# Splitting the first stage of a fused attention and gated-product kernel into two passes through DRAM

## The chip, the cores and the metric

The kernel runs on one core of a Trainium2 chip. The metric is the device time of one execution in microseconds (us). Three runs of the kernel before took 1695.24, 1697.13 and 1695.3 us; the median is 1695.3 us.

## What is computed

The reference, cut to what matters (8 batches, 8 heads, 576 positions, 64 columns a head; 4608 tokens of 512 columns; widths 1024 and 1536):

```python
k_p, v_p = mean of k, v over groups of 8 positions        # 72 keys
attn = softmax(q @ k_p.T / 8)                             # 576 x 72 per head
x = attn @ v_p, heads side by side                        # 4608 x 512
h = (x @ w1) * (x @ w2)                                   # 4608 x 1024
y = h @ w3 @ w_out                                        # 4608 x 512
xn = y / sqrt(mean(y*y) + 1e-6) * rms_g
out = (silu(xn @ w_gate) * (xn @ w_val)) @ w_out2         # 4608 x 512
```

The weights and the MoE inputs arrive as 64-bit floats, so every weight is converted on the chip.

## The kernel before, in words

**Products.** Every large product is made of three matmuls (`mm3`, lines 86 to 89): both operands are split into a high part (rounded to the matmul's type) and a low part (the rest), and high by high, high by low and low by high are summed in PSUM. A split (`split`, lines 82 to 84) is one copy on ACT and one subtraction on DVE. The 4608 tokens are worked on in 9 blocks of 512 (index i, `NB`), the 1024 columns of h in 8 strips of 128 (index m, `KF1`).

**Prelude.** w3 @ w_out is folded into one matrix first (lines 540 to 583): w3 is loaded, converted (`Conv`, lines 97 to 154), transposed on PE and multiplied by w_out. The result, split, stays in SBUF as `wph` and `wpl` (four tiles of pool `wC`) for the whole first stage. A list of side steps, `aux`, is laid between these matmuls: the attention of batch 0, the conversion of the first half of w1 and w2, and the gate products of strips 0 to 3 of block 0 (`ab0`), kept in SBUF as `hf0`.

**First stage.** `ab(i, m, s)` (lines 633 to 642) is 12 matmuls: strip m of x @ w1 (s = 0, then ACT copies it out) or of x @ w2 (s = 1, then DVE multiplies it by the copy); the product h is split into `hh`, `hl`. `y_mm(i, m)` (through `second`, lines 462 to 471) is another 12 matmuls: strip m of h times the folded matrix, into four PSUM banks that gather over the 8 strips. `Pipe.run` (lines 654 to 675) walks m: gate products of strip m, then `y_mm` of strip m-1, and after each piece a tick of a `Ticker`. The ticks spread the attention of the next batch over the block: `att_of(i)` (lines 644 to 652) is a list of some 35 short steps for 20 ticks. A block thus has 288 product matmuls, 192 of gate products and 96 of the second product. When the 8 strips are done, `y_end` (lines 586 to 626) copies y to `ydram`, and squares and sums it for the norm.

**Attention.** For each of 5 tiles of 128 positions (the last 64): `step_Q` transposes q on PE; `step_S` (two halves) multiplies by the pooled keys on PE, takes the maximum on DVE, and makes 4 exponentials a half on ACT; `step_N` divides on DVE; `step_T` transposes the result, on PE for batches 0 and 1, and for the others with 12 block transposes on DVE a full tile (lines 340 to 347). `av_step` multiplies by the pooled values and writes the split x of the next block. `pool_four` and `pool_sum` load and pool k and v.

**Second stage, weights.** w_gate and w_val are converted, combined into 8 forms (`gv_jobs`, lines 744 to 794, function `sums`: four subtractions, and for each of two column halves a split of 128x1024 and two writes to `wdram` on the POOL queue), 12 groups in all. This and the conversion of w_o2 (`o2_jobs`) are the list `prep`, ticked through during blocks 7 and 8 of the first stage and the start of the second (lines 1129 to 1138). `ring_load` brings the forms back from `wdram`, `o2_load` w_o2.

**Second stage, products.** Block 0 is computed plainly (`gv`, `o_mm`; lines 1139 to 1171), then pairs of blocks through `quad` and `o_part` to the end.

**Order.** Each engine works in one order; SP and POOL issue DMAs in order, so an issue that waits for a buffer or for data holds up those behind it. The framework's scheduler turns the program's order into the engines' orders by its own plan, so a step can move a little.

Of the kernel before, what the change touches and what calls it, by code (L numbers as in the profile page):

```python
# [1 line left out]

# [18 lines left out]
def kernel(  # L21
# [17 lines left out]


    nc = tc.nc
# [30 lines left out]

    def ftile(dt=F32):
        return f_p.tile([P, 512], dt, tag="f", name="f")
# [15 lines left out]

# [91 lines left out]
    rdram = dram_p.tile([NB, TB], F32, name="rdram")  # L182
    ones_f = const.tile([P, 1], F32, name="ones_f")
# [3 lines left out]


# [48 lines left out]
    def att_steps(b):  # L237
# [14 lines left out]
        def step_k1():  # L252
            load_q(0)
# [3 lines left out]
            load_q(1)  # L257

        def step_kT():
            ps = psum()  # L260
            kp = st8.pop(("kp", b))
            for p in range(NP):
                nc.tensor.transpose(
                    ps[:, p * SP : (p + 1) * SP], kp[:, p * P : (p + 1) * P], ident[:SP, :SP]
                )
            pv = ps[:, : NP * SP].rearrange("d (p s) -> d p s", p=NP)
            nc.scalar.activation(kT[:D, :, :SP], pv[:D], AF.Copy, scale=ATT_SCALE)
            nc.scalar.activation(kT[D:, :, SP:], pv[D:], AF.Copy, scale=ATT_SCALE)

        def step_Q(g, hf):  # L270
# [8 lines left out]
            if hf < nu:  # L279
                ps = psum()  # L280
# [13 lines left out]
        def step_S(t, hf):  # L294
            s0, n = TILES[t]
            ps = psum()
# [38 lines left out]
        def step_T(t, hf):  # L335
# [12 lines left out]
            ps = psum()  # L348
# [15 lines left out]

        pre = [step_k0, step_k1]
        steps = [step_kT, lambda: step_Q(0, 0), lambda: step_Q(0, 1)]
        for t in range(NTL):

            def a(t=t):
                step_S(t, 0)  # L370

            def bq(t=t):
                step_Q(t // 2 + 1, t % 2)

            def c(t=t):
                step_S(t, 1)

            def d(t=t):
                if t > 0:
                    step_T(t - 1, 0)  # L380
                step_N(t)

            def e(t=t):
                if t > 0:
                    step_T(t - 1, 1)

            steps += [a, bq, c, d, e]
        steps[4:4] = [load_v]
        steps[11:11] = [step_v]
        steps += [lambda: step_T(NTL - 1, 0), lambda: step_T(NTL - 1, 1)]  # L390
        return pre, steps

    def av_step(b, i, p):
# [4 lines left out]
        ps = psum()  # L398
# [63 lines left out]
    def second(i, m, wh, wl, last, tok_major):  # L462
        hh, hl = h_t.pop((i, m))
        if m == 0:
            yacc[i] = [py_p.tile([P, 512], F32, tag="y", name="y") for _ in range(4)]
# [37 lines left out]
    hf0 = [preA_p.tile([P, 512], F32, name=f"hf0_{m}") for m in range(4)]  # L503
# [26 lines left out]
    def ab0(m, s):  # L530
        xh, xl = xtile(0)
        if s == 0:
            nc.scalar.copy(hf0[m], mm_feat(w1h, w1l, xh, xl, m))
        else:
            pb = mm_feat(w2h, w2l, xh, xl, m)
            nc.vector.tensor_tensor(out=hf0[m], in0=pb, in1=hf0[m], op=ALU.mult)
# [11 lines left out]
    aux = atts[0][0] + atts[0][1][:-2] + c0[:2] + atts[0][1][-2:]  # L548
# [3 lines left out]
    aux += [lambda m=m, s=s: ab0(m, s) for s in range(2) for m in range(4)]  # L552
    aux += atts[1][0]
# [5 lines left out]
    for n in range(NW3):  # L559
# [73 lines left out]
    def ab(i, m, s):  # L633
        wh, wl = ((w1h, w1l), (w2h, w2l))[s]
        ps = mm_feat(wh, wl, *xtile(i), m)
        if s == 0:
            a0[i, m] = ftile()
            nc.scalar.copy(a0[i, m], ps)
        else:
            hf = ftile()  # L640
            nc.vector.tensor_tensor(out=hf, in0=ps, in1=a0.pop((i, m)), op=ALU.mult)  # L641
            split_h(i, m, hf)

    def att_of(i):
        steps = av_steps(i, i + 1)
        if i + 1 < B:
            steps = steps + atts[i + 1][1][:-2]
            if i + 2 < B:
                steps = steps + atts[i + 2][0]
            steps = steps + atts[i + 1][1][-2:]  # L650
            steps = steps + av_steps(i + 1, i + 1)
        return steps

    class Pipe:


        def __init__(self):
            self.pend, self.todo = None, []

        def fin(self):  # L660
            if self.pend is not None:
                self.todo += self.pend()
                self.pend = None

        def run(self, i, ms, wide, second, tick):
            for m in ms:
                for s in range(2):
                    wide(i, m, s)
                    if self.todo:
                        self.todo.pop(0)()  # L670
                    tick()
                self.fin()
                tick()
                self.pend = lambda m=m: second(i, m)
            tick.flush()

    pipe = Pipe()
    c1 = conv_steps([load_w12(n) for n in range(8, 16)], 2)
    for m in range(4):
        split_h(0, m, hf0[m])  # L680
        y_mm(0, m)
    preB.close()
    preA.close()
    x1_p = ctx.enter_context(tc.tile_pool(name="x1", bufs=1))
    wA_p = ctx.enter_context(tc.tile_pool(name="wA", bufs=4))
    pools[1] = x1_p
    col_tiles(wA_p, W12, (w1h, w1l, w2h, w2l))
    cv = Ticker(c1, 1)
    cv.run(6)
    tick = Ticker(att_of(0), 14)  # L690
    for m in range(4, KF1):
        ab(0, m, 0)
        cv.step()
        tick()
    cv.flush()
    for m in range(4, KF1):
        ab(0, m, 1)
        tick()
        pipe.fin()
        tick()  # L700
        pipe.pend = lambda m=m: y_mm(0, m)
    tick.flush()
    xt.pop(0)

    for i in range(1, NB - 2):
        pipe.run(i, range(KF1), ab, y_mm, Ticker(att_of(i), 3 * KF1 - 4))
        xt.pop(i)

    for st in att_of(NB - 2):
        st()  # L710
    att.close()
    r_p = ctx.enter_context(tc.tile_pool(name="r", bufs=5, side="right"))

# [25 lines left out]
    o2r = {}  # L739

    def rtile(nm, dt=F32R):
        return r_p.tile([P, 2048], dt, tag="r", name=nm)

    def gv_jobs(G, s, kp):
        cell = {}
        w = (w_gate, w_val)[s]

        def quart(z):
            if "f" not in cell:
                cell["f"] = rtile("wf", F32).rearrange("p (j f c) -> p j f c", j=2, f=8)  # L750
# [3 lines left out]
        def sums(_):  # L754
            f = cell.pop("f")

            def q(n):
                return f[:, :, FI[n], :]

            for o, x, y in (  # L760
# [5 lines left out]
                nc.vector.tensor_tensor(out=q(o), in0=q(x), in1=q(y), op=ALU.subtract)  # L766
            for j in range(2):
                c = 2 * G + j
                st = rtile("wst").rearrange("p (f l c) -> p f l c", f=8, l=2)
                nc.scalar.copy(st[:, :, 0, :], f[:, j])  # L770
                nc.vector.tensor_tensor(
                    out=st[:, :, 1, :],
                    in0=f[:, j],
                    in1=st[:, :, 0, :].bitcast(F32),
                    op=ALU.subtract,
                )
                for z in range(2):
                    nc.gpsimd.dma_start(
                        out=wdram[s, c, z][:, :, kp],
                        in_=st[:, 4 * z : 4 * z + 4].bitcast(F32),  # L780
                    )
                ready.add((s, c, kp))

        def view(z):
            return z.rearrange("p (j f c) -> p j f c", j=2, f=2)

        def src(z):
            k0 = (2 * z + kp) * P
            return w[k0 : k0 + P, G * 512 : (G + 1) * 512]

        return [
            Conv(src(0), raw_p, out=lambda: quart(0), view=view),
            Conv(src(1), raw_p, out=lambda: quart(1), view=view, then=sums),
        ]

    def o2_jobs(g):
# [7 lines left out]
        def done(_):  # L804
            f = cell.pop("f")
            hi, lo = o2r[g] = [wtile(wC_p, nm) for nm in ("oh", "ol")]
            split(hi, lo, f)
            nc.gpsimd.dma_start(out=odram[g][0], in_=hi.bitcast(F32))
            nc.gpsimd.dma_start(out=odram[g][1], in_=lo.bitcast(F32))

        return [
            Conv(
                w_o2[(4 * g + j) * P : (4 * g + j + 1) * P, :],
                raw_p,
# [5 lines left out]

    prep = []
    for G in range(3):
        for s in range(2):
            for kp in range(2):
                prep += gv_jobs(G, s, kp)
    for g in range(3):
        prep += o2_jobs(g)
    for j, cv_ in enumerate(prep):
        cv_.on_act = True
        if j % 5 > 2:  # L830
            cv_.pool = (r_p, "xq", 2)
    prep = conv_steps(prep, 4)

# [22 lines left out]
    o2_n = [3]  # L856
# [13 lines left out]
    def xn_load(i, c):  # L870
        if c == 0:
            xr[i] = ftile()
            nc.sync.dma_start(out=xr[i], in_=rdram[i].partition_broadcast(P))
        r = raw_p.tile([P, 1024], I32, tag="raw", name="raw").bitcast(F32)
        xr[i, c] = r.rearrange("p (k t) -> p k t", k=2)
        nc.sync.dma_start(
# [353 lines left out]
```

## Time and profile before

| what | us or share |
|---|---|
| median of 3 runs | 1695.3 |
| profiled execution: span from first to last instruction | 1693.5 |
| profiled execution's own time: the span with some 1.8 us around it, by the runs | about 1695.3 |
| PE busy | 1619.1 (96%) |
| DVE busy | 1037.3 (61%) |
| ACT busy | 663.9 (39%) |
| POOL busy | 90.8 (5%) |
| DMA, mean over the span | 159 GB/s |

How to read it: PE's busy time is a union of matmuls that overlap each other, so it tells where PE had nothing at all to do, not how densely it ran; a lone matmul of 128x512 shows some 0.39 us, yet in a dense stretch they start every 0.23 us. The count of matmuls in a stretch and its length say more. DVE and ACT shares are close to what they say, as their instructions hardly overlap.

### The profile page before, as it was taken

What the parts mean: (1) busy time and instruction counts of PE and PEld (TensorE: products, weight loads), DVE (VectorE), ACT (ScalarE), POOL (GpSimd) and SP (SyncE); (2) the same over time, 40 slices, a digit from 0 to 9 for tenths busy, and PEclk for the clock granted to TensorE, in tenths of its full rate; (3) what the DMA queues carried; (4) which work ended last, traced back from release to release, by engine and by line L of the source; (5) the groups of instructions that cost most, each with busy time, mean ns of one, the idle gap of its engine ahead of it and who ended that gap; (6) DMA issues with size and microseconds to landing.
All of it is one profiled execution on the core that took longest, in us unless ns stands there. A gap on an engine that the chain in (4) does not pass through costs nothing.

```text
span 1693.5 us, 19782 instructions
## 1 busy us (share of the span) xinstructions
PE 1619.1 (96%) x7252; PEld 1275.7 (75%) x7252; DVE 1037.3 (61%) x1850; ACT 663.9 (39%) x1604; POOL 90.8 (5%) x104
## 2 busy tenths in 40 slices
PE   6898999999999999998798999999999999999999
PEld 3466677777777778776676888888888888888887
DVE  7875475757585858677756653476355735465344
ACT  3654543334333334455543243243333334233321
POOL 0001010100000000031310000000000000000000
PEclk9999999999999999999999999999999999999999
DMA  9854340413131310297968774367455746455422
GB/s 261 217 144 100 47 102 28 82 34 77 39 71 44 65 48 6 84 323 257 334 223 328 286 270 159 141 247 253 164 194 186 257 165 224 149 201 212 182 101 75
DMA packets 125588, 270.07 MB, mean 159 GB/s; under 512 B 50858, under 2 KB 77482, under 8 KB 109364
## 3 DMA queue, kind: packets, MB, share of 16 engines
q1 hardware_dynamic: 104916, 227.89, 39.8%
q0 software_dynamic: 20576, 40.92, 9.4%
q8 instruction: 57, 0.93, 0.2%
q14 instruction: 39, 0.32, 0.1%
HBM read 218.39 MB, written 50.37 MB: 159 GB/s over the span
## 4 chain that ended last, share of the span: by engine, by line
PE 47%; DMA 3%; DVE 0%; ACT 0%; issue 0%; SPq 0%; ACTq 0%
PE ps L87 9%; PE ps L88 9%; PE ps L89 9%; PE o L89 5%; PE o L88 5%; PE o L87 5%; DMA wr<-wd 2%; PE y L88 2%; PE y L89 2%; PE y L87 2%; DMA raw<-in_moe_w_out_dram 0%; DMA ydram<-f 0%; DVE f L596 0%; DVE hl L84 0%; ACT f L591 0%
## 5 line engine op out<-in xcount | busy, mean ns | idle before, releaser
L87 PE MATMUL ps<-xf,wr 128*128 128x512 f32 x576 | 224.1, 389 | 0.0
L89 PE MATMUL ps<-xf,wr 128*128 128x512 f32 x576 | 224.1, 389 | 0.0
L88 PE MATMUL ps<-xf,wr 128*128 128x512 f32 x576 | 224.1, 389 | 0.0
L89 PE MATMUL o<-oh,hcl 128*128 128x512 f32 x384 | 149.6, 389 | 0.0
L87 PE MATMUL o<-oh,hch 128*128 128x512 f32 x384 | 149.4, 389 | 0.0
L88 PE MATMUL o<-ol,hch 128*128 128x512 f32 x384 | 149.4, 389 | 0.0
L1029 ACT COPY f<-ps 128x512 f32<-128x512 f32 x144 | 84.4, 586 | 163.2 <-PE ps L89 158.1
L343 DVE STREAM_TRANSPOSE aT<-s 32x256 f32<-32x256 f32 x324 | 140.9, 435 | 5.5
L315 ACT ACTIVATE s<-ps,mx 128x72 f32<-128x72 f32 (+1 forms) x320 | 98.1, 323 | 107.0 <-DVE mx L312 106.9
L87 PE MATMUL y<-hh,wph 128*128 128x512 f32 x288 | 120.8, 420 | 16.5 <-ACT hh L83 9.2
L87 PEld LDWEIGHTS ps<-xf,wr 128*128 128x128 f32 x576 | 108.1, 188 | 22.6 <-ACT f L1029 0.2
L89 PEld LDWEIGHTS ps<-xf,wr 128*128 128x128 f32 x576 | 108.1, 188 | 22.5
L88 PEld LDWEIGHTS ps<-xf,wr 128*128 128x128 f32 x576 | 108.1, 188 | 22.3
L87 PE MATMUL ps<-xh,w2h 128*128 128x512 f32 x288 | 117.9, 410 | 6.8 <-DVE f L641 3.6
L1033 DVE TENSOR_TENSOR f<-y,f 128x512 f32<-128x512 f32 x48 | 33.2, 691 | 144.4 <-PE y L89 144.4
L88 PE MATMUL y<-hl,wph 128*128 128x512 f32 x288 | 115.9, 402 | 4.2 <-DVE hl L84 4.0
L87 PE MATMUL ps<-xh,w1h 128*128 128x512 f32 x288 | 115.9, 402 | 2.4 <-ACT s L315 2.2
L89 PE MATMUL y<-hh,wpl 128*128 128x512 f32 x288 | 114.6, 398 | 0.0
L83 ACT CAST hh<-f 128x512 fp32r<-128x512 f32 x80 | 49.4, 618 | 161.7 <-DVE f L641 121.5
L89 PE MATMUL ps<-xh,w2l 128*128 128x512 f32 x288 | 112.8, 392 | 0.0
L88 PE MATMUL ps<-xl,w2h 128*128 128x512 f32 x288 | 112.6, 391 | 0.0
L88 PE MATMUL ps<-xl,w1h 128*128 128x512 f32 x288 | 112.6, 391 | 0.0
(154 smaller groups left out, 3113.6 us busy)
## 6 DMA issues: line engine op xcount, KB each, us to landing
wr<-wd SPq DMA_DIRECT2D x96, 1024.0 KB
wd<-wst POOLq DMA_DIRECT2D x48, 512.0 KB, 6.6
raw<-in_moe_w_dram SPq DMA_DIRECT2D x32, 512.0 KB
wr<-wd SPq DMA_DIRECT2D x24, 512.0 KB
oh<-od SPq DMA_DIRECT2D x12, 1024.0 KB
ol<-od SPq DMA_DIRECT2D x12, 1024.0 KB
raw<-in_moe_w_out_dram SPq DMA_DIRECT2D x20, 512.0 KB
ydram<-f SPq DMA_DIRECT2D x36, 256.0 KB
```

Of the source, the lines that this page charges most:

```text
L83: nc.scalar.copy(hi, src)
L87: nc.tensor.matmul(o, lh, rh, start=first, stop=False, skip_group_check=part)
L88: nc.tensor.matmul(o, lh, rl, start=False, stop=False, skip_group_check=part)
L89: nc.tensor.matmul(o, ll, rh, start=False, stop=last, skip_group_check=part)
L315: nc.scalar.activation(s_t[t][:n, h, :SP], pv[:, j, :], AF.Exp, bias=mx[:, j, :], accum_out=den_t[t][:n, h, :],)
L343: nc.vector.transpose(aT[32 * kb : 32 * kb + 32, :, s0 + 32 * i : s0 + 32 * i + 32], s_t[t][32 * i : 32 * i + 32, :, 32 * kb : 32 * kb + 32],)
L1029: nc.scalar.copy(t, bank)
L1033: nc.vector.tensor_tensor(out=t, in0=bank, in1=t, op=ALU.add)
```

## The change

1. The first stage is made in two passes. `ab` no longer splits h; it writes each strip (128x512, 256 KB) to the new `hdram` by an SP DMA. The second product of all 9 blocks comes after the last gate product, in a loop of its own that loads h two strips at a time, splits 128x1024 at once, and runs `second` 72 times in a row. Its PSUM banks alternate between two pools from block to block.
2. `wph` and `wpl` are written to DRAM (`wpdram`, four POOL DMAs of 1 MB) when they are made, and loaded again (SP) in block 8. That frees pool `wC` during the first pass.
3. Weight preparation (`gv_steps`, in place of `gv_jobs`) uses `wC` for its tiles and becomes 85 steps spread over 116 ticks, one tick after each `ab` of blocks 1 to 7 and the first four of block 8. w_o2's conversion goes to the second pass.
4. The attention steps have fixed places in the 16 `ab` of a block (`positions`), in bursts: tile t's two score halves and a transpose of q after the odd one, 2t+1; the transposes of tile t-1 and the division of tile t after 2t+2. Attention's PSUM banks come from pool `py` instead of `ps`.
5. `ab0` goes; strips 0 to 3 of block 0 use `ab`, in the order m, then s.

The diff, cut to its core:

```diff
+    hdram = [dram_p.tile([KF1, P, TB], F32, name=f"hd{i}") for i in range(NB)]
+    wpdram = [dram_p.tile([2, P, 4, 512], F32, name=f"wpd{g}") for g in range(2)]
+    def apsum():
+        if att_py:
+            return py_p.tile([P, 512], F32, tag="y", name="pa")
+        return psum()
...
+    def ab(i, m, s):
+        wh, wl = ((w1h, w1l), (w2h, w2l))[s]
+        ps = mm_feat(wh, wl, *xtile(i), m)
+        if s == 0:
+            a0[i, m] = ftile()
+            nc.scalar.copy(a0[i, m], ps)
+        else:
+            hf = hxtile("hh" if m % 2 else "hl").bitcast(F32)
+            nc.vector.tensor_tensor(out=hf, in0=ps, in1=a0.pop((i, m)), op=ALU.mult)
+            nc.sync.dma_start(out=hdram[i][m], in_=hf)
...
+            nc.gpsimd.dma_start(out=wpdram[g][0], in_=wph[g].bitcast(F32))
+            nc.gpsimd.dma_start(out=wpdram[g][1], in_=wpl[g].bitcast(F32))
...
+    def positions(i):
+        pos = [[] for _ in range(2 * KF1)]
+        b = i + 1
+        if b >= B:
+            return pos
+        A = atts[b]
+        pos[1] = av_steps(i, i + 1) + [
+            lambda: A.S(0, 0), lambda: A.Q(1, 0), lambda: A.S(0, 1)
+        ]
+        pos[2] = [lambda: A.N(0), A.load_v]
+        for t in range(1, NTL):
+            p = 2 * t + 1
+            pos[p] += [lambda t=t: A.S(t, 0)]
+            if t < 4:
+                pos[p] += [lambda t=t: A.Q(1 + t // 2, t % 2)]
+            pos[p] += [lambda t=t: A.S(t, 1)]
+            pos[p + 1] += [
+                lambda t=t: A.T(t - 1, 0), lambda t=t: A.T(t - 1, 1), lambda t=t: A.N(t)
+            ]
+        pos[8] += [A.v]
+        pos[12] += [lambda: A.T(NTL - 1, 0), lambda: A.T(NTL - 1, 1)]
+        pos[13] += av_steps(b, i + 1)
+        if b + 1 < B:
+            C = atts[b + 1]
+            pos[9] += [C.k0]
+            pos[10] += [lambda: C.q(0)]
+            pos[13] += [C.k1, lambda: C.q(1)]
+            pos[15] += [C.kT, lambda: C.Q(0, 0), lambda: C.Q(0, 1)]
+        return pos
...
+    prep = Ticker(gv_prep, 2 * KF1 * (NB - 2) + 4)
+    for i in range(1, NB):
...
+        pos = positions(i)
+        for n, (m, s) in enumerate((m, s) for m in range(KF1) for s in range(2)):
+            ab(i, m, s)
+            for st in pos[n]:
+                st()
+            prep()
+            if i == NB - 1 and n == 5:
+                prep.flush()
...
+                        nc.sync.dma_start(out=lst[g].bitcast(F32), in_=wpdram[g][l])
...
+    def h_load(n):
...
+            nc.sync.dma_start(
+                out=hr[n].rearrange("p (k t) -> p k t", k=2),
+                in_=hdram[i][2 * g : 2 * g + 2].rearrange("k p t -> p k t"),
+            )
+    def h_split(n):
+        if n < NH:
+            t = wtile(wA_p, "hb").rearrange("p (l k) t -> p l (k t)", l=2)
+            hb[n] = t
+            split(t[:, 0], t[:, 1], hr.pop(n))
...
+    for i in range(NB):
+        for m in range(KF1):
+            n = i * (KF1 // 2) + m // 2
+            if m % 2 == 0:
+                h_load(n + 3)
+                h_split(n + 2)
...
+            second(i, m, wph[m // 4][:, c, :], wpl[m // 4][:, c, :], KF1 - 1, False)
...
+        todo = y_end(i)
+    side.flush()
...
+    o2_load(1)
```

## Rows read from the trace of the kernel before

**Rows 1.** The page's first part: busy us (share) x instructions

```profile
span 1693.5 us, 19782 instructions
...
PE 1619.1 (96%) x7252; PEld 1275.7 (75%) x7252; DVE 1037.3 (61%) x1850; ACT 663.9 (39%) x1604; POOL 90.8 (5%) x104
```

**Rows 2.** By stretch: length, engines' busy us (x count), PEclk, DMA share, GB/s

```profile
0.00:125.20 125.20, 105.44 (x409) 59.95 (x409) 97.85 (x209) 66.44 (x176) 8.88 (x14) 1.00 0.77 208
125.20:201.00 75.80, 63.43 (x319) 48.49 (x317) 39.01 (x81) 34.99 (x126) 8.32 (x7) 0.93 0.44 82
201.00:698.70 497.70, 484.21 (x2335) 377.15 (x2333) 330.68 (x709) 194.05 (x721) 29.19 (x25) 1.00 0.23 51
698.70:854.80 156.10, 140.70 (x582) 110.79 (x581) 119.41 (x205) 84.01 (x129) 38.24 (x50) 0.96 0.84 289
854.80:968.40 113.60, 104.00 (x437) 82.80 (x436) 74.17 (x104) 42.75 (x61) 6.21 (x8) 0.97 0.77 276
968.40:1693.50 725.10, 721.34 (x3181) 596.54 (x3179) 376.22 (x545) 241.65 (x391) 0.00 (x0) 1.00 0.51 187
366.50:449.30 82.80, 80.22 (x388) 62.86 (x387) 55.01 (x118) 31.56 (x119) 5.89 (x5) 1.00 0.26 57
```

**Rows 3.** Groups on PE, 366.5 to 449.3 us: busy us, mean ns | idle before

```profile
L300 PE MATMUL ps<-kT,qT 128*128 128x144 f32 (+1 forms) x40 | 6.6, 288 | 0.0
L401 PE MATMUL ps<-aT,vp 72*64 72x256 f32 x32 | 4.3, 392 | 0.0
L282 PE MATMUL ps<-ident,q 128*128 128x128 f32 (+1 forms) x20 | 2.8, 268 | 0.7 <-ACT s L315 0.7
```

**Rows 4.** Groups on DVE, the same block

```profile
L343 DVE STREAM_TRANSPOSE aT<-s 32x256 f32<-32x256 f32 x54 | 23.5, 435 | 0.9
L84 DVE TENSOR_TENSOR hl<-f,hh 128x512 fp32r<-128x512 f32 x8 | 5.5, 692 | 2.6 <-ACT hh L83 2.5
L641 DVE TENSOR_TENSOR f<-ps,f 128x512 f32<-128x512 f32 x8 | 5.5, 688 | 10.1 <-PE ps L89 10.0
L312 DVE TENSOR_REDUCE mx<-ps 128x4 f32<-128x288 f32 (+1 forms) x10 | 4.5, 446 | 0.9 <-PE ps L300 0.8
L328 DVE TENSOR_TENSOR s<-s,den 128x576 f32<-128x576 f32 (+1 forms) x5 | 3.8, 756 | 0.2
...
L227 DVE TENSOR_TENSOR kv<-kv 72x512 f32<-72x512 f32 x4 | 2.7, 686 | 5.7 <-DMA kv<-in_k_dram 3.4 <-DMA kv<-in_v_dram 2.3
L599 DVE TENSOR_TENSOR f<-f 128x512 f32<-128x512 f32 x3 | 2.1, 684 | 0.7 <-ACT f L591 0.7
L596 DVE COPY f<-y 128x512 f32<-128x512 f32 x2 | 1.4, 691 | 0.2 <-ACT f L591 0.2
...
L607 DVE TENSOR_TENSOR f<-f 128x512 fp32r<-128x512 f32 x1 | 0.7, 682 | 0.0
```

**Rows 5.** Groups on DVE, 690 to 968.4 us: weight preparation

```profile
L771 DVE TENSOR_TENSOR wst<-wf,wst 128x1024 fp32r<-128x1024 f32 x24 | 28.7, 1222 | 1.8 <-ACT wst L770 1.7
L142 DVE SCALAR_TENSOR_TENSOR raw<-raw 128x512 int32<-128x512 int32 x33 | 22.3, 686 | 9.2 <-ACT raw L126 9.2
...
L766 DVE TENSOR_TENSOR wf<-wf 128x256 f32<-128x256 f32 x48 | 18.3, 417 | 0.1
L150 DVE CUSTOM_DVE_ANT_0 wf<-raw,f 128x1024 uint16<-128x1024 uint16 x24 | 16.3, 687 | 2.0 <-DMA wd<-wst 1.8
L137 DVE TENSOR_SCALAR f<-f 128x512 int32<-128x512 int32 x36 | 15.6, 433 | 14.6 <-ACT f L128 14.6
```

**Rows 6.** Timeline of DVE, back to back: start us, length us

```profile
399.83 1.29 DVE L227 TENSOR_TENSOR kv<-kv 72x512 f32<-72x512 f32 x2
401.04 0.68 DVE L641 TENSOR_TENSOR f<-ps,f 128x512 f32<-128x512 f32 x1
```

**Rows 7.** Timeline of PE after a gap

```profile
133.65 0.79 PE L87 MATMUL y<-hh,wph 128*128 128x512 f32 x1 [4.83 <-DVE wpl L84]
```

**Rows 8.** Chain that ended last: start us, us, what

```profile
868.95 4.78 DMA wr<-wd
```

More of the change, by code (lines that the diff above doesn't have):

```diff
@@ L464, in second @@
         if m == 0:
[L465 removed]
+            yacc[i] = [ybank(i) for _ in range(4)]
         for t in range(4):
@@ L654 @@
[L654 to L712, printed above, removed]
+    def ybank(i):
+        if i % 2:
+            return psum()
+        return py_p.tile([P, 512], F32, tag="y", name="y")
@@ L775, in sums @@
+                    in0=f[:, :, FI[x], :],
+                    in1=f[:, :, FI[y], :],
                     op=ALU.subtract,
                 )
[L777 to L787, printed above, removed]
-            k0 = (2 * z + kp) * P
-            return w[k0 : k0 + P, G * 512 : (G + 1) * 512]
@@ L791, in gv_jobs, with put @@
-        return [
-            Conv(src(0), raw_p, out=lambda: quart(0), view=view),
-            Conv(src(1), raw_p, out=lambda: quart(1), view=view, then=sums),
-        ]
+        def put(j):
+            f = cell["f"]
+            c = 2 * G + j
+            st = ptile("wst").rearrange("p (f l c) -> p f l c", f=8, l=2)
+            split(st[:, :, 0, :], st[:, :, 1, :], f[:, j])
+            for z in range(2):
+                nc.gpsimd.dma_start(
+                    out=wdram[s, c, z][:, :, kp],
+                    in_=st[:, 4 * z : 4 * z + 4].bitcast(F32),
+                )
+            ready.add((s, c, kp))
@@ new lines, in gv_steps @@
+        cs = []
+        for z in range(2):
+            k0 = (2 * z + kp) * P
+            src = w[k0 : k0 + P, G * 512 : (G + 1) * 512]
+            cs.append(Conv(src, raw_p, out=lambda z=z: quart(z), view=view))
+            cs[z].on_act = True
+        return cs, [
+            lambda: (cs[1].s0(), cs[0].s1()),
+            cs[0].s2,
+            cs[1].s1,
+            cs[1].s2,
+            sums,
+            lambda: put(0),
+            lambda: put(1),
+        ]
+    groups = [gv_steps(G, s, kp) for G in range(3) for s in range(2) for kp in range(2)]
@@ new lines @@
+    c1 = conv_steps([load_w12(n) for n in range(8, 16)], 2)
+    preB.close()
+    preA.close()
+    x1_p = ctx.enter_context(tc.tile_pool(name="x1", bufs=1))
+    wA_p = ctx.enter_context(tc.tile_pool(name="wA", bufs=4))
+    pools[1] = x1_p
+    col_tiles(wA_p, W12, (w1h, w1l, w2h, w2l))
+    att_py.append(1)
+    cv = Ticker(c1, 1)
+    cv.run(6)
+    pos = positions(0)
+    pos[0] += [atts[1].kT, lambda: atts[1].Q(0, 0), lambda: atts[1].Q(0, 1)]
+    half = [pos[2 * n] + pos[2 * n + 1] for n in range(KF1)]
@@ L805, in done @@
             f = cell.pop("f")
[L806 to L811, printed above, removed]
+            hl = [rtile(nm).rearrange("p (j c) -> p j c", j=4) for nm in ("of", "of")]
+            split(hl[0], hl[1], f)
+            for l in range(2):
+                nc.gpsimd.dma_start(out=odram[g][l], in_=hl[l].bitcast(F32))
+        js = [
             Conv(
                 w_o2[(4 * g + j) * P : (4 * g + j + 1) * P, :],
-                raw_p,
+                (r_p, "xq", 2),
                 out=lambda j=j: row(j),
@@ L819, in o2_jobs @@
         ]
[L821 to L832, printed above, removed]
+        for j in js:
+            j.on_act = True
+        return js
     SEQ = [(c, s) for c in range(NCH) for s in range(2)] * (1 + NB // 2)
@@ L1160 @@
         if c == 0:
-            for st in pipe.todo:
-                st()
+            while todo:
+                todo.pop(0)()
+        if c == 3:
+            o2_load(2)
         ring_load(0, 2 * c + 3)
```

252 lines of the change are left out of this document (152 added, 100 removed).

## The prediction

> **What bounds the kernel now.** I read the page's first part, then the busy times cut by stretch, then the groups of one block. PE is busy 96% of the span [rows 1], so a gain can only come out of the rest and out of stretches where PE runs thinly. In the last stretch 3181 matmuls take 725.1 us, 0.228 us each, with PE idle for 4 us [rows 2]: that is PE at its pace, and the measure for the others. The change makes no product matmul fewer. Per stretch [rows 2]: from 698.7 to 968.4 us, 582 + 437 = 1019 matmuls take 269.7 us, where 1019 x 0.228 = 232.3 would do, so 37.4 us are lost, at a DMA share of 0.84 and 0.77 and a granted clock of 0.96 and 0.97. From 201.0 to 698.7 us, six blocks take 82.95 us each: 288 products x 0.228 = 65.7 us and 17.3 us more, of which 13.7 us is the attention's own PE work (6.6 + 4.3 + 2.8) [rows 3]. Only 3.6 us a block is loose there. From 125.2 to 201.0 us the clock is 0.93, behind a gap of 4.83 us [rows 7].
>
> The stretch to watch is the six blocks: DVE works 55.0 us in 82.8, two thirds [rows 2]. The change takes 96 matmuls out of each block and puts weight preparation in.
>
> **The sum, part by part**, against the profiled span of 1693.5 us.
>
> *Prelude.* The four writes of the folded matrix are 4 MB on POOL's queue; the first 2 MB fall amid the weight loads. At the stretch's 208 GB/s [rows 2] they are 10 us of transfer, in a stretch whose DMA share is 0.77, so between 0 (the unused 23% takes them) and +10 us. I take +4. The h writes of four strips are 1 MB on SP behind loads already issued: 0, covered by the matmuls of the next strip, 12 x 0.228 = 2.7 us.
>
> *Block 0.* The second product there waited 4.83 us for DVE's split of the folded matrix [rows 7]; it moves away. But the next gate products need the second half of w1, converted by the same two engines: that wait is next. From 75.8 us, clock included (7% of it, 5.3 us), at best 4.8 + 5.3 = 10 us go; at worst the conversion is late by 3 us more. I take -5.
>
> *Six blocks, PE.* 192 x 0.228 = 43.8 us plus the attention's 13.7 us is 57.5 us: the floor. What stands against it is the block before less what moves away: 82.95 - 96 x 0.228 (21.9) - 0.5 for the norm's two matmuls = 60.55 us. So were PE alone to decide, bursts bring 3 us a block at most.
>
> *Six blocks, DVE.* Of 55.0 us, the split of h (5.5), and y's sums, copies and split (2.1 + 1.4 + 0.7) go [rows 4]; the tiny rest is left in, so 45.3 us stay. Preparation comes: 28.7 + 18.3 + 16.3 us, and 24 conversions' two other steps, 24 x (0.686 + 0.433) = 26.9, 90.2 us in all [rows 5]; 16 of 116 ticks make 12.4 us a block. DVE then has 57.7 us, as much as PE. And it lies unevenly. Behind gate products 3 to 10 of 16 (counted from 0) stand 48 of the 54 transposes (20.9 us), four products of h (2.8), eight maxima (3.6), four divisions (3.0), half the pooling (1.4) [rows 4] and half the preparation (6.2): 37.9 us. PE needs there 96 x 0.228 = 21.9 us, eight of ten score halves (5.3) and three of five transposes of q (1.7) [rows 3]: 28.9 us. The other half has 28.6 us of PE over 19.8 of DVE.
>
> PE can run ahead of DVE by the four banks that gate products use, four pieces of 2.7 us. But at place 13 the products of attention and pooled values wait for the last transposes of place 12, and behind them on PE's queue stand gate products. With nothing carried over that edge a block is 37.9 + 28.6 = 66.5 us, and with the waits for DMA and ACT that DVE already has in such a block (5.7 for pooled loads, 2.6 behind ACT [rows 4], of which I count about 3.5) 70 us. The bounds are 57.5 and 70.
>
> Here a row has a say on DVE's pace. Two pooling sums together take 1.29 us, and the instruction after them starts 1.21 us after the first [rows 6]: 0.60 us apart, though each lasts 0.69 [rows 4]. Some twenty such pairs in the heavy half would save 1.5 us, so its upper end is 68.5 and the middle is 63. The two ends are equally far from any row, for before has no block in which DVE is the limit; I take the middle. Price: 63 - 60.55 = 2.45, six times: +15 us. The Trainium skill says otherwise (VectorE: DVE Perf Modes, section "The DRAIN you can't avoid"): the next instruction does not start until the pipe is empty. By it the middle would be 63.75 and the price +19; by the row it is +15, and the row decides.
>
> *Queues in these blocks.* On SP, each h write waits for DVE's product and holds the loads issued behind it: raw weights, q and pooled inputs, placed three or more places (8 us) ahead, so I cost it at 0; if that cover goes, it is ACT's conversions and the scores behind them that wait. On POOL, 48 weight writes come between the adding loads of k and v (rival 4). DMA: 51 GB/s now [rows 2]; h adds 2 MB a block (33 GB/s) and the preparation, 3 MB a group, some 80 GB/s, below the 187 GB/s of the last stretch with its full PE [rows 2].
>
> *Blocks 7 and 8, the second pass, the start of stage two.* Without conversions PE should run at its pace; the sum of matmuls is unchanged. In the second pass 512 KB of h come per 24 matmuls, 5.5 us: 96 GB/s, under those 187; the split of 1024 columns is 1.22 us of DVE [rows 5] in 5.5. So 0, covered by PE. w_o2's conversion lies there too, and has room. Of the 37.4 us lost now I leave two waits: one like the 4.78 us for the first forms [rows 8], since w_o2's 4 MB now are loaded at that point, and about 2 us at the hand-over from gate products to h. So -31; with half of today's waits left, -18; with none, -37.
>
> *Last stretch:* the same work, 0.
>
> Sum: 4 - 5 + 15 - 31 = -17, a span of 1676.5; with the 1.8 us around it, **1678 us**. The profiled execution stood at the median of 1695.3.
>
> **The rivals.**
>
> 1. *DVE is never the limit.* Blocks stand at PE's 57.5 us: six times 3.05 is -18 for +15; 1676.5 - 33 = 1643.5, so 1645 us. For it: DVE's 57.7 us is a sum of lengths that overlap [rows 6], and the banks carry 11 us. Against: no engine but PE has run so full here.
> 2. *PE stands before place 13 (slower).* The products there wait for transposes in each of six blocks; a block is 70 us, +57 for +15: 1720 us. It decides from 60.55 + (31 + 5 - 4) / 6, about 66 us a block. For: 37.9 against 28.9 us in the heavy half. Against: PSUM allows the gate products behind to go first, if the planner sees it.
> 3. *The late waits stay* (the change doesn't do what it is written to do): loads of 4 MB of folded matrix, then 4 MB of w_o2, keep PE waiting as conversions did: -18 for -31, so 1691 us, and with a block of 65 us 1703.
> 4. *POOL's queue.* The adding loads of k and v stand behind weight writes that wait for DVE; DVE waits 5.7 us a block for pooled inputs now [rows 4]. Doubled, it is +34: 1712 us. The Trainium skill (SBUF — State Buffer, the box on DVE blocking DMA) has it that some DVE instructions lock POOL out of writing descriptors, which speaks against moving such writes into a DVE-bound stretch; no row here shows that lock.
>
> **Chances.** Forecast (a block of 60.5 to 66.5 us) 0.45; rival 1 0.25; rival 2 0.17; rival 3 0.07; rival 4 0.06. A measurement can tell 0.2% (3.4 us) from no change. Faster by more: all of rival 1, 0.35 of the forecast's 0.45, 0.02 of rival 3: 0.62. Slower: rivals 2 and 4, 0.05 of the forecast's upper end, 0.04 of rival 3: 0.32. Between: 0.06. The range, from rival 1's end to a block of 69 us: 1648 to 1714; the forecast's own is 1664 to 1700.
>
> **What would show it.** Six blocks of about 63 us, DVE busy near 90% in them, PE's waits there for DVE (products of h, transposes) and no longer few; blocks 7 and 8 at 44 us each; then 864 matmuls in about 200 us at a clock of 1.00; first-stage y writes all in that pass; the stretch before the last one free of waits for `wr`. A block under 60 us shows rival 1, of 66 or more rival 2; PE idle at `wr` or `oh` rival 3; DVE idle at `kv` rival 4. The prediction is wrong if DVE's share in the blocks stays under 80% while PE has gaps.

## The result, and the profile after

The changed kernel took 1711.98 us (median of 4 runs, 1708.68 to 1718.17) against 1695.27 us: a ratio of 1.0099, 95% interval [1.0077, 1.012]. It is slower, where the forecast was 1678 us and faster.

The page's first part, after [rows 1]:

```profile
span 1716.4 us, 19990 instructions
## 1 busy us (share of the span) xinstructions
PE 1623.1 (95%) x7250; PEld 1296.5 (76%) x7250; DVE 1021.8 (60%) x1813; ACT 658.3 (38%) x1567; POOL 95.0 (6%) x107
```

PE is busy 4 us longer than before and DVE 16 us less, and 22.9 us more pass. The windows by stretch, after [rows 2], show where. In order: prelude; second half of block 0; the six attention blocks; blocks 7 and 8; the second pass; the first products of stage two; the rest.

```profile
core 0: us, PE busy (x) PEld busy (x) DVE busy (x) ACT busy (x) POOL busy (x), PEclk, DMA share, GB/s
0.00:133.00 133.00, 109.16 (x420) 62.97 (x420) 96.80 (x206) 65.74 (x175) 9.93 (x17) 0.97 0.77 208
133.00:188.70 55.70, 43.73 (x231) 32.43 (x232) 33.61 (x75) 33.83 (x125) 7.09 (x7) 0.88 0.77 186
188.70:588.00 399.30, 358.56 (x1736) 285.98 (x1734) 326.69 (x735) 180.22 (x681) 53.63 (x59) 0.94 0.56 154
588.00:675.20 87.20, 87.20 (x387) 72.19 (x386) 28.98 (x46) 19.87 (x32) 7.65 (x11) 1.00 0.66 229
675.20:887.00 211.80, 203.88 (x881) 165.67 (x880) 119.92 (x153) 96.01 (x133) 14.64 (x13) 0.98 0.60 204
887.00:991.20 104.20, 99.04 (x423) 80.88 (x422) 39.84 (x57) 21.02 (x34) 2.01 (x2) 0.97 0.66 232
991.20:1716.40 725.20, 721.49 (x3181) 596.41 (x3179) 375.95 (x545) 241.61 (x391) 0.00 (x0) 1.00 0.51 187
```

- **Six blocks:** 399.3 / 6 = 66.55 us each, against the neutral 60.55: **+36 us**.
- **Late stretches:** 87.2 + 211.8 + 104.2 = 403.2 us for 387 + 881 + 423 = 1691 matmuls. Before, 1019 of them took 269.7 us [rows 2]; the other 672 are second products that moved here from blocks 0 to 6 (and a few of the norm's matmuls), at 0.228 us another 153.2. So 403.2 - 422.9 = **-20 us**.
- **Prelude and block 0:** the remainder, 22.9 - 36 + 20 = **+7**. PE stood once there, 9.3 us, for DVE's division (`s`, L327). That is not the change's steady price: in a later kernel with the same code up to there (e11) the six blocks began at 180.1 us instead of 188.7, and this profiled execution is the longest of the four, 6.2 us over their median.
- The last stretch is the same: 725.2 us.

So the six blocks decide. A block is 358.56 / 6 = 59.8 us of busy PE and 6.8 us of idle PE. The largest waits there, PE's and then DVE's (line and releaser: total, times, longest; PE's other three, 4.2 us in all, are for DVE too):

```profile
PE pa L299 <- DVE xl L412: 23.7, 5, 6.3
PE pa L262 <- DVE kp L231: 12.8, 7, 4.2
...
DVE kv L228 <- DMA kv<-in_v_dram: 38.7, 10, 8.0
DVE raw L143 <- ACT raw L127: 8.9, 5, 3.9
```

PE stands at the scores (L299), whose PSUM bank waits for DVE's low part of x (`xl`, L412), and DVE stands at v's pooled loads. One such place, early in the second attention block (from 249.2 us), in the timeline of DVE, then PE (start, length, engine, line, operation, [idle before <- releaser]):

```profile
258.31 0.69 DVE L228 TENSOR_TENSOR kv<-kv 72x512 f32<-72x512 f32 x1 [2.53 <-DMA kv<-in_v_dram]
258.92 0.68 DVE L540 TENSOR_TENSOR hl<-ps,f 128x512 f32<-128x512 f32 x1
261.78 0.69 DVE L228 TENSOR_TENSOR kv<-kv 72x512 f32<-72x512 f32 x1 [2.19 <-DMA kv<-in_v_dram]
262.39 0.88 DVE L412 SCALAR_TENSOR_TENSOR xl<-pa,xh 128x192 fp32r<-128x192 f32 x3
```

```profile
257.54 0.40 PE L94 MATMUL ps<-xl,w1h 128*128 128x512 f32 x1
262.79 1.09 PE L299 MATMUL pa<-kT,qT 128*128 128x144 f32 x3 [4.85 <-DVE xl L412]
```

v's pooling has place 8 in the program and `xl` place 1, but in DVE's order, as the scheduler made it, the pooling comes first. DVE waits for v, `xl` waits in its queue, the scores wait for `xl`, and gate products wait behind the scores. A second price follows. The windows around that gap, in the columns of the stretches above:

```profile
257.90:262.80 4.90, 0.05 (x2) 0.01 (x1) 2.31 (x5) 0.00 (x0) 0.54 (x1) 0.85 1.04 290
262.80:265.00 2.20, 2.20 (x9) 2.19 (x10) 1.57 (x6) 0.00 (x0) 0.00 (x0) 0.50 1.01 362
265.00:267.00 2.00, 2.00 (x7) 1.73 (x7) 0.73 (x2) 1.99 (x12) 0.00 (x0) 0.50 0.91 240
267.00:270.00 3.00, 3.00 (x12) 2.45 (x11) 1.83 (x5) 1.61 (x9) 0.00 (x0) 0.80 0.77 228
270.00:273.00 3.00, 3.00 (x20) 2.64 (x19) 2.31 (x6) 0.67 (x1) 0.66 (x1) 1.00 0.04 11
```

After 4.9 us of standing, PE's granted clock is 0.50 (1.2 GHz) for 4.2 us and 0.80 on the mean of the next 3: 4.2 x 0.5 + 3 x 0.2 = 2.7 us lost on top of the 4.85.

### The profile page after: what moved, and what is told of

It reads as the page before. It is cut to its first block, busy times and chain, and to the rows that moved or that the text cites. A ratio compares the mean times of both kernels' runs of the same rounds, so it can differ in the third digit from the quotient of the medians.

```text
span 1716.4 us, 19990 instructions
## 1 busy us (share of the span) xinstructions
PE 1623.1 (95%) x7250; PEld 1296.5 (76%) x7250; DVE 1021.8 (60%) x1813; ACT 658.3 (38%) x1567; POOL 95.0 (6%) x107
## 4 chain that ended last, share of the span: by engine, by line
PE 68%; DMA 11%; DVE 11%; issue 7%; ACT 2%; POOL 1%; SPq 0%; POOLq 0%; ACTq 0%; DVEq 0%
PE ps L93 14%; PE ps L94 14%; PE ps L95 14%; PE o L95 5%; PE o L94 5%; PE o L93 5%; DMA kv<-in_v_dram 5%; DVE aT L342 3%; PE y L93 2%; PE y L94 2%; PE y L95 2%; DMA raw<-in_moe_w_dram 2%; PE pa L299 2%; DMA raw<-in_moe_w_out_dram 1%; DMA ydram<-f 1%
## 5 line engine op out<-in xcount | busy, mean ns | idle before, releaser
L93 PE MATMUL ps<-xh,w1h 128*128 128x512 f32 x288 | 123.2, 428 | 0.1
L1071 DVE TENSOR_TENSOR f<-y,f 128x512 f32<-128x512 f32 x48 | 33.2, 691 | 143.1 <-PE y L95 143.1
L314 ACT ACTIVATE s<-pa,mx 128x72 f32<-128x72 f32 (+1 forms) x280 | 85.2, 330 | 80.3 <-DVE mx L311 80.3
L95 PE MATMUL ps<-xh,w1l 128*128 128x512 f32 x288 | 114.9, 401 | 0.1
L93 PE MATMUL ps<-xh,w2h 128*128 128x512 f32 x288 | 112.5, 391 | 1.9 <-DVE hh L540 1.7
L127 ACT ACTIVATE raw<-raw 128x512 int32<-128x512 uint32 x76 | 51.8, 683 | 127.1 <-DMA raw<-in_moe_w_dram 35.4
L1153 DVE TENSOR_TENSOR acc<-o,acc 128x512 f32<-128x512 f32 x64 | 43.5, 689 | 75.5 <-PE o L95 75.0
L95 PEld LDWEIGHTS o<-oh,hcl 128*128 128x128 f32 x384 | 72.1, 188 | 15.4 <-DVE hcl L1093 0.6
```

The source lines that it names most:

```text
L93: nc.tensor.matmul(o, lh, rh, start=first, stop=False, skip_group_check=part)
L95: nc.tensor.matmul(o, ll, rh, start=False, stop=last, skip_group_check=part)
L127: nc.scalar.activation(self.low, low_u, AF.Copy, scale=2.0**-29)
L314: nc.scalar.activation(s_t[t][:n, h, :SP], pv[:, j, :], AF.Exp, bias=mx[:, j, :], accum_out=den_t[t][:n, h, :],)
L1071: nc.vector.tensor_tensor(out=t, in0=bank, in1=t, op=ALU.add)
L1153: nc.vector.tensor_tensor(out=a, in0=ys[j], in1=a, op=ALU.add)
```

## The experiments

Block times below are means over blocks 1 to 6, from the first matmul of one to that of the next, in the profiled execution. The changed kernel has 66.5. Theory 1: the loads of v come late, because k, v and the raw weights share three buffers and two queues. Theory 2: DVE has too much to do in these blocks, too unevenly. Each ratio is against runs of the kernel before on the same chip, with a 95% interval; its median was 1694.6 to 1697.0 us throughout. Of each edit the lines that matter are shown; `...` marks what is left out.

### What the preparation costs in all: e2

```diff
-    prep = Ticker(gv_prep, 2 * KF1 * (NB - 2) + 4)
+    prep = Ticker(gv_prep, 2 * KF1 + 4)
...
-            prep()
+            if i >= NB - 2:
+                prep()
```

> Weight preparation leaves the six blocks with attention and is done, whole, beside blocks 7 and 8. Both theories expect shorter blocks, as both the work on DVE (12.4 us a block) and the sharing of the three raw buffers go; theory 1 expects v's waits on DVE to fall from 38.7 to about 10 us and blocks of 60 to 61 us, theory 2 blocks of 58 to 60 us with v's waits hardly smaller. Blocks 7 and 8 then carry 90 us more of DVE beside 29 in 87 us, so they should take about 120 us together, and the run lands near 1712 - 38 + 33 = 1707.

1730.06 us, ratio 1.0208 [1.0167, 1.0248]. The six blocks:

```profile
181.70:534.60 352.90, 342.82 (x1735) 269.94 (x1733) 270.57 (x621) 140.36 (x622) 22.67 (x20) 1.00 0.39 92
```

58.8 us a block, of it 57.1 of busy PE at a clock of 1.00: bursts and two passes alone gain 1.7 us a block over the neutral 60.55, and the floor of 57.5 was right. So the preparation costs 66.5 - 58.8 = 7.7 us a block, 46 us in all. Beside blocks 7 and 8 it costs more: 148.4 us for 87.2, where about 120 was expected, so the run missed its 1707. It does not tell the theories apart, as DVE's work, ACT's conversions, the shared buffers and the weight writes all go at once: DVE's waits for v fall to 11.3 us, as theory 1 has it, those for k grow from 1.2 to 27.5, and the blocks are as short as theory 2 has it.

### v's loads: e1, e5, e8, e7

```diff
-        pos[2] = [lambda: A.N(0), A.load_v]
+        pos[2] = [lambda: A.N(0)]
...
-        pos[8] += [A.v]
+        pos[3] += [A.v]
...
+            pos[14] += [C.load_v]
...
```

> Only v's load and pooling move: the load goes from place 2 to place 14 of the block before, the pooling from place 8 to place 3. Theory 1 (DVE stands in its order at v's pooling, whose second load lands late, and what PE waits for stands behind it): DVE's 38.7 us of waits for v in the six blocks fall under 12, PE's 23.7 us in front of the first scores under 8, a block goes from 66.5 to 61 to 63 us, the run from 1712 to 1680 to 1692. Theory 2 (DVE has simply too much work, and would idle somewhere else): blocks stay at 65 to 67 us, the run within 6 us of the changed kernel.

1705.81 us, 1.0058 [1.0038, 1.0078]; blocks 65.4. DVE's wait for v falls only from 38.7 to 29.9 us, PE's for `xl` stays at 24.6: the edit did not take the wait away, so it decides little.

e5 loads the raw weights into a tile of pool `wC` instead of the shared `raw`:

```diff
...
-            cs.append(Conv(src, raw_p, out=lambda z=z: quart(z), view=view))
+            cs.append(Conv(src, lambda z=z: rawt(z), out=lambda z=z: quart(z), view=view))
```

> The preparation's raw loads take a tile of pool wC instead of the three raw buffers, so that in blocks 1 to 6 the pooled loads of k and v have those to themselves; DVE's work is the same. Theory 1, in its new form (the sharing of the three buffers makes v late, and DVE stands at it): DVE's waits for v fall from 38.7 us in the six blocks to under 12, PE's 23.7 us in front of the first scores to under 8, a block goes from 66.5 to 61 to 63 us, the run from 1712 to 1683 to 1692. Theory 2 (the amount of work on DVE, 57.7 us a block, unevenly placed): a block stays at 65 to 66 us, as the idle time moves to the end of the block, where PE waits for DVE's pooling of k.

1703.67 us, 1.0055 [1.0033, 1.0077]; blocks 65.0. The waits for v are gone, and DVE waits 27.7 us for k instead. e8 is e5 with e1:

> Own raw tile and v's load moved to the block before, nothing else. Theory 1: v's waits vanish (under 5 us in the six blocks), blocks of 61 to 62 us, 1680 to 1688. Theory 2: 65 us a block as in the run that moved v alone.

1707.31 us, 1.0068 [1.0048, 1.0089]; blocks 65.0. e7 adds the earlier conversion of w_o2 (e4, below):

> Own raw tile, v's load moved to the block before, and the last weight's conversion beside blocks 7 and 8. By theory 1 the gains add: blocks of 61 to 62 us (-30), block 0's second half 5 us shorter, the second pass 12 us shorter for 5 more in blocks 7 and 8, so 1672 to 1682, under the kernel before. By theory 2 it is 1693 to 1700.

1697.42 us, 1.0006 [0.9992, 1.002]; blocks 64.5, second pass 199.8. The wait that theory 1 names can be taken away, and 1.5 us a block come back (e5). But a wait for k took its place, so these runs price v's wait alone, not late loads as such.

### DVE's work: e3, e6, e9, e10

e3 makes all attention transposes on PE, with copies by ACT:

```diff
-            if b >= 2:
+            if b >= B:
```

> The transposes of the attention of batches 2 to 7 go from DVE (23.5 us a block) to PE (40 more short matmuls, about 4.5 us a block, with copies on ACT). Theory 2: with 32 us of work left on DVE, blocks come to PE's 60 to 62 us, whatever v does. Theory 1: v's waits stay, PE still loses some 20 us in front of the first scores, and blocks stay at 65 to 67 us.

1702.91 us, 1.004 [1.0025, 1.0055]; blocks 64.9. A miss for theory 2 as stated. DVE's new waits are for k (46.1), v (33.3) and ACT's exponentials (38.7); PE waits 11.4 for the divided `s`, is busy 61.7 us of each block, and no longer waits for `xl`. e6 is e3 with e5:

> Own raw tile for the preparation, and the transposes of attention on PE for all batches: neither cause is left. PE's floor rises from 57.5 to about 62 us by its 40 transposes a block. If the two causes are all there is, a block takes 61 to 63 us, DVE is busy for half of it, and the run lands at 1680 to 1692. If blocks stay at 65, something else stands in the way, such as ACT, which makes the copies.

1706.74 us, 1.0052 [1.0031, 1.0073]; blocks 64.6, with PE busy 60 to 63 of them: with all transposes PE is busy 4 to 5 us longer a block than in e2, so these two runs say little on what DVE's work is worth.

e9 keeps the preparation out of the heavy half:

```diff
-            prep()
+            if i >= NB - 2 or not 3 <= n <= 10:
+                prep()
+                if i < NB - 2:
+                    prep()
```

> The preparation steps stand only behind gate products 0 to 2 and 11 to 15 of each of the six blocks (two at a time, the same number a block), none in places 3 to 10, where v's and k's pooling, the k split and the norms already fill DVE. If the uneven placing is the cause (theory 2), the heavy half of a block falls from 37.9 us of DVE work to about 31.7, the blocks from 66.5 to 60 to 62 us each and the run to about 1685 us. If v's pooled loads are (theory 1), or the sum of DVE's work whatever its order, the blocks stay at 65 to 67 us and the run at about 1712.

1701.88 us, 1.0056 [1.0037, 1.0076]; blocks 65.6. The placing within a block, by itself, is not most of it. e10 leaves only half of the steps in the six blocks:

```diff
-    prep = Ticker(gv_prep, 2 * KF1 * (NB - 2) + 4)
+    prep = Ticker(gv_prep[:42], 2 * KF1 * (NB - 3))
+    prep_b = Ticker(gv_prep[42:], 2 * KF1 + 6)
...
+            prep.flush()
+            prep = prep_b
```

> 42 of the 85 preparation steps stand beside the six blocks, the other 43 beside blocks 7 and 8. DVE has some 5 us less in each of the six blocks. With preparation costing 7.7 us a block (66.5 with it, 58.8 without), half of it should leave about 62.5 us a block, 24 us less in all; blocks 7 and 8 go from 87 to about 90 us if DVE has the room there, and the run comes to about 1690 us. If blocks 7 and 8 have no room, they take 20 us more and the run stays at about 1710.

1699.2 us, 1.0023 [1.0, 1.0045]; blocks 62.6, blocks 7 and 8 96.6. Half the preparation, half the price (58.8, 62.6, 66.5). DVE is busy 50.3 us a block instead of 54.4, yet its waits for v stay (42.6 us): what of the preparation counts, this run does not say.

### The second pass: e4, e11

e4 converts w_o2 beside blocks 7 and 8:

```diff
+            side = Ticker(conv_steps(o2, 1), 3 * KF1)
...
+            if r_p is not None:
+                side()
```

> The conversion of the last weight moves from the second pass to blocks 7 and 8. If its loads and copies hold up ACT and DVE in front of the norm's sums, the second pass goes from 211.7 to about 203 us and the run from 1712 to about 1703. If the 11 us lost there come from the writes of y and their tiles, the pass stays at 209 to 212.

1702.92 us, 1.0044 [1.0024, 1.0065]. The second pass falls from 211.8 to 199.8 us and blocks 7 and 8 grow from 87.2 to 92.0. e11 leaves the conversion and issues the norm's matmul two places later:

```diff
-        return [sq_split, lambda: None, rms]
+        return [sq_split, lambda: None, lambda: None, lambda: None, rms]
```

> In the second pass the norm's matmul stands two places later behind the split of its squares, so PE should not wait for ACT's squares, which wait for the raw load of w_out. If these waits are what the second pass loses, it falls from 211.8 to 203 to 205 us and the run to about 1704. If the conversion of w_o2 holds PE by other waits (eviction by ACT or DVE), the second pass stays at 210 to 212 us.

1700.41 us, 1.0047 [1.0025, 1.0068]; the second pass, to 0.3 us before the first matmul of stage two:

```profile
666.60:868.70 202.10, 199.84 (x880) 163.26 (x879) 120.44 (x153) 96.24 (x133) 12.10 (x13) 1.00 0.66 219
```

The changed kernel's waits there were:

```profile
PE ps L673 <- ACT f L665: 4.4, 1, 4.4
PE y L673 <- ACT f L665: 3.0, 1, 3.0
```

PE stood at the norm's matmul for the split squares (`f`, L665) on ACT, which in this pass waited 22.9 us for the raw w_out of its conversions; two places are cover enough, and the clock comes back to 1.00.

### The queues: e13, and e14 against e15

e12, the first try at a better version, joined e5, e9, e10 and e11:

> Raw loads of the preparation in a tile of their own, steps only in the light places, half of them beside blocks 7 and 8, and the later norm. If the blocks' cost is the uneven load of DVE together with the shared raw buffers, the six blocks come to 59 to 60 us each, the second pass to 204 and the run to 1665 to 1675 us, below both kernels. If what is left is PE's and ACT's own chain (scores, exponentials) as in the run with a raw tile of its own, the blocks stay at 63 or more and the run at about 1690.

1703.61 us, 1.0067 [1.0047, 1.0088]; blocks 65.5, a miss and 3 us worse than e10. DVE waits 25.9 us for ACT's conversions, two steps of which now come at a time, and 33.2 us for k (3.1 and 5.1 in e10). On POOL's queue there, weight writes waited 209 us for DVE's splits, with k's adding loads behind them; on SP, the writes of h. That is rival 4's mechanism, so e13 is meant to take the hold-ups out, with the whole preparation left in: a raw tile of its own, and both kinds of writes issued later.

```diff
...
-            nc.sync.dma_start(out=hdram[i][m], in_=hf)
+            h_out.append(lambda: nc.sync.dma_start(out=hdram[i][m], in_=hf))
+            while len(h_out) > (i > 0):
+                h_out.pop(0)()
...
+            e = 1 + 7 * n + 5 + j + 2
+            if e < len(gv_prep):
+                gv_prep[e] = lambda f=gv_prep[e]: (f(), writes.pop(0)())
```

> Whole preparation in the six blocks, but the queues set free: raw weights in a tile of their own, each write of h issued two places later on SP, each weight write two steps later on GpSimd. If the queues are the cause, VectorE's waits for k and v (6.5 us a block) go and a block falls from 66.5 us to 58 to 60 us: run about 1670. If VectorE's own work and its placing are the cause, PE's waits for VectorE stay and a block takes 64 to 66 us: run about 1705.

1703.61 us, 1.0037 [1.0008, 1.0066]; blocks 64.2. The queues did not come free: weight writes waited 147.1 us for DVE's splits on POOL's queue (99.1 in the changed kernel), and DVE waits 27.0 us for k and 2.5 for v. PE's waits have moved:

```profile
PE pa L265 <- DVE xl L415: 9.3, 4, 2.6
PE pa L302 <- DVE xl L415: 9.0, 3, 3.8
PE pa L302 <- ACT s L317: 6.4, 3, 2.8
```

e14 and e15 both have half the preparation (e10) and the later norm (e11); e14 has the later writes as well.

> Half the preparation beside blocks 7 and 8, the later norm, and the two kinds of writes issued later (raw buffers shared as before). Against e15, which has the first two alone: if the queues are what is left, the blocks fall from 62.5 to 58 to 60 us, run about 1672; if not, they stay at 62 to 63, run about 1689.

> Half the preparation beside blocks 7 and 8 and the later norm together. Their gains lie in different stretches and should add: blocks 62.5, second pass 202.5, span 1690.4 - 9 = 1681, run 1683 to 1690 us, below the kernel before. If the raw load of w_out is late for another reason when blocks 7 and 8 are denser, the second pass stays at 211 and the run at 1699.

e14: 1678.48 us, 0.9905 [0.9872, 0.9938]; blocks 62.2. e15: 1684.0 us, 0.9936 [0.9912, 0.996]; blocks 62.7. So e10 and e11 add up and beat the kernel before; the later writes give half a microsecond a block. But the later writes changed no hold-up either (weight writes waited 132.0 us for DVE's splits in e14, 130.4 in e15; DVE 40.6 and 43.5 us for v). What held queues cost thus stays untested.

### Work and room together: e16, e17, e18

e16 is e15 with the transposes of two of the five tiles on PE:

```diff
-            if b >= 2:
+            if b >= 2 and t % 2 == 0:
```

> As e15, and the transposes of tiles 1 and 3 of each block's five on PE and ACT: VectorE has some 9 us less a block (of 23.5), PE about 2 us more. If VectorE's work is the limit, a block falls from 62.5 to 59 to 60 us, run about 1670. If the waits for k and v decide whatever VectorE does, the blocks stay at 62 to 63 and the run at about 1689.

**1659.92 us, 0.9794 [0.9758, 0.983]**: the fastest kernel of this study, below both. Its six blocks, and PE's waits in them:

```profile
177.50:531.70 354.20, 350.31 (x1832) 280.24 (x1830) 245.83 (x548) 178.72 (x682) 42.02 (x44) 1.00 0.54 144
```

```profile
PE pa L349 <- DVE s L327: 3.7, 3, 2.7
PE pa L262 <- DVE xl L412: 0.2, 1, 0.2
```

59.0 us a block at a clock of 1.00, with DVE busy 41.0 us, 9.3 less than in e15. Loads, writes and buffers are as in e15, yet DVE's waits for v fall from 43.5 to 8.0 us and PE's for `xl` from 24.4 to 0.2. So the late loads were, here, mostly an effect of DVE's load; that a DVE which is ahead frees the shared buffers early, and so brings the loads early, is the likely link, and no run shows it by itself.

e17 keeps all the preparation in the blocks (of e16's edits only the transposes and the later norm), e18 is e16 with 63 of the 85 steps in them.

> The changed kernel with the transposes of tiles 1 and 3 on PE and ACT, and the later norm; all the preparation stays in the six blocks, queues and raw buffers as the change has them. VectorE's 55 us a block become some 46 (half of what moving all transposes takes away). If VectorE's work was the cause, a block falls from 66.5 to 59 to 61 us and blocks 7 and 8 stay at 87: run 1650 to 1665. If the preparation costs by its queues and shared raw buffers as well, the blocks stay at 63 to 65 us, run about 1680.

> As e16, with 63 of the 85 steps in the six blocks and 22 beside blocks 7 and 8. If VectorE has room, blocks of 59.5 us and 90 us for blocks 7 and 8: some 1 us less than e16, 1655 to 1662. If the room was just used up at half the preparation, blocks of 61 to 62 and a run of about 1672.

e17: 1677.27 us, 0.9882 [0.9835, 0.9929]; blocks 62.4, between the two forecasts. Moving two tiles' transposes off DVE is thus worth 66.5 - 62.4 = 4.1 us a block, set against the 7.7 of the preparation. e18: 1681.26 us, 0.9926 [0.9897, 0.9955]; blocks 63.6, slower than e16 and no faster than e17: a miss. Its first four blocks:

```profile
179.60:238.10 58.50, 58.17 (x307) 46.41 (x305) 42.72 (x94) 30.55 (x116) 7.79 (x8) 1.00 0.59 153
238.10:306.60 68.50, 60.08 (x307) 48.87 (x305) 47.61 (x102) 31.57 (x117) 10.85 (x12) 0.93 0.63 174
306.60:366.10 59.50, 58.06 (x308) 46.71 (x306) 41.68 (x93) 30.63 (x116) 7.81 (x8) 1.00 0.56 148
366.10:433.00 66.90, 59.70 (x307) 48.40 (x305) 47.12 (x102) 31.58 (x118) 10.84 (x12) 0.95 0.65 179
```

They alternate. 63 steps are 10.5 a block, one and a half groups of seven, so every other block has DVE work for a second group (47 us for 42), PE stands (8.4 us for `xl` in the second, 7.2 in the fourth), and the clock falls. At the start of the second, DVE, then PE:

```profile
244.87 0.69 DVE L228 TENSOR_TENSOR kv<-kv 72x512 f32<-72x512 f32 x1 [6.79 <-DMA kv<-in_v_dram]
...
249.80 2.36 DVE L90 TENSOR_TENSOR wst<-wf,wst 128x1024 fp32r<-128x1024 f32 x2 [1.11 <-ACT wst L89]
```

```profile
253.68 0.61 PE L299 MATMUL pa<-kT,qT 128*128 128x144 f32 x1 [8.42 <-DVE xl L412]
```

DVE stood 6.8 us for v, then worked and waited 7.8 us more, mostly on the preparation, and only then came `xl`: late load and amount of work add up in one stand. That the grouping makes the difference is argued from these rows; no run changed it alone, and e10 and e15, with one whole group in every block, have uneven blocks too (55.8 to 66.0 us in e10).

**The runs side by side.** Us a block, and DVE's waits for k and v in all six:

| run | block | PE idle | DVE busy | ACT busy | waits for k and v |
|---|---|---|---|---|---|
| changed kernel | 66.5 | 6.8 | 54.4 | 30.0 | 39.9 |
| e5 | 65.0 | 5.8 | 54.8 | 29.6 | 29.9 |
| e3 | 64.9 | 3.2 | 33.7 | 34.6 | 79.4 |
| e13 | 64.2 | 5.3 | 54.9 | 29.5 | 29.5 |
| e18 | 63.6 | 4.4 | 44.6 | 31.3 | 45.7 |
| e15 | 62.7 | 4.3 | 50.2 | 27.4 | 48.8 |
| e17 | 62.4 | 3.3 | 45.8 | 32.0 | 32.7 |
| e16 | 59.0 | 0.6 | 41.0 | 29.8 | 12.0 |
| e2 | 58.8 | 1.7 | 45.1 | 23.4 | 38.8 |

PE's idle time mostly falls with DVE's work, but the work alone does not order the runs: at some 45 us of it a block takes 58.8 us without preparation (e2) and 62.4 to 63.6 with it (e17, e18). Nor do the waits for k and v: in e2 they are as long as in the changed kernel, and PE hardly stands.

**What stays open.** That the preparation beside attention costs the 7.7 us is shown (e2), and that a lighter DVE gives much of it back (e17: 4.1 us; e16 against e15: 3.7 of the 3.9 then left). How the rest divides between DVE's own steps, ACT's conversions, shared buffers and held queues is not shown; e13's 2.4 us are a raw tile of its own (1.5 alone, e5) and later issues together, and e13's and e17's edits were not run together.

## Why the prediction was wrong, step by step

- *Floor, blocks 7 and 8, last stretch:* right. 57.1 us of PE a block (57.5), 43.6 us a block (44), 725.2 us. Bursts gain 1.7 us of at most 3.
- *"The middle is 63 ... I take the middle. Price ... +15 us":* the step that failed. It measured 66.5 us, +36, by itself more than the whole forecast gain. The sum of DVE's work was near (59.0 us as a sum of lengths, 57.7 predicted; 54.4 busy, as they overlap), and it is DVE that PE waits for, in all 40.7 us of its idle time. Two terms were mis-sized. DVE's own waits were counted at "about 3.5" us a block; it idles (399.3 - 326.7) / 6 = 12.1 us, 6.5 for v alone. And PE's stands were priced at their length; at the clock of 0.94, busy PE took 59.8 us for the 57.1 of e2, so each block pays 2.7 us more, a term that the sum for these blocks put at nothing. 57.1 + 2.7 + 6.8 idle = 66.6. That 37.9 + 28.6 gave 66.5 as well is luck: that sum stands on an edge at place 13 where PE did not wait (and counts three transposes of q in places 3 to 10, where two stand).
- *Where PE stands:* rival 2 put it "before place 13", at the transposes. It gave the number (it "decides from ... about 66 us a block") but not the place: PE stands at places 1 and 15, for `xl` and for k's pooling. The transposes matter as work, not as the thing waited for. By the prediction's own signs a block of 66 or more shows rival 2, and DVE idle at `kv` (39.9 of its 72.6 idle us) rival 4; neither holds as it was worked out.
- *The heavy half:* the argument of 37.9 against 28.9 us pointed at places 3 to 10; taking the preparation out of these (e9) gave 0.9 us of 7.7. The placing within a block is not what decided.
- *"Queues ... I cost it at 0", rival 4:* its 1712 us are what was measured, by luck: the waits for k and v did not double (5.7 us a block before, 6.7 after). Yet before they were covered by an idle DVE, and now PE stands behind one of them in DVE's order. What held queues cost is not known, as e13 and e14 did not free them. k's and v's adding loads land no later with a busier DVE: 5.6 and 5.3 us in the six blocks, 6.6 and 6.7 before. So nothing here shows the lock that the Trainium skill (SBUF — State Buffer, the box on DVE blocking DMA) describes.
- *DVE's pace:* the row goes on deciding. At the end of the first attention block `kp`'s sum starts at 247.02, lasts 0.41, and the next instruction starts at 247.35: they overlap. The Trainium skill (VectorE: DVE Perf Modes, "The DRAIN you can't avoid"), from which the prediction took only that the next instruction waits for an empty pipe, adds there that one which is not held starts earlier; this row agrees with that.

```profile
247.02 0.41 DVE L231 TENSOR_TENSOR kp<-kv 72x256 f32<-72x256 f32 x1
247.35 0.68 DVE L143 SCALAR_TENSOR_TENSOR raw<-raw 128x512 int32<-128x512 int32 x1
```

- *Late stretches, "-31":* -20. "w_o2's conversion lies there too, and has room" failed: DVE and ACT had room by their sums, but ACT's order put the squares behind a conversion that waited for a load. Issuing the norm's matmuls two places later gave 9.4 us (e11: 202.4 us to the first matmul of stage two, for 211.8).
- *Prelude and block 0, "4 - 5":* they lost about 7 together in the profiled execution, with one stand of 9.3 us for DVE; in e11 they ended 8.6 us earlier, so about -2. The two cannot be told apart.

## What to carry to other kernels

Before work is moved into a stretch to use an engine's idle time, take from that idle time the waits the engine already has: an engine that keeps 45 us of work and 6 us of waits has no 12 us to give once the stretch shrinks to 60. Then price each stand of PE at its length and the slow clock behind it. And when an engine is near full, late loads may be its effects: lighten the engine first (here the transposes of two tiles of five, and half of the preparation), then look at the queues again.

## What was not expected of the hardware

A stand of 4.9 us cost another 2.7 by the clock: 0.50 for 4.2 us and then up to 1.00 by 270 us, while PE was busy without a break. In e18 the blocks whose only stand was 0.2 or 1.4 us ran at 1.00 (58.5 and 59.5 us), those with one of 8.4 and 7.2 us at 0.93 and 0.95 (68.5 and 66.9 us): the step from 58.5 us is larger than the stand.
